# A quarter of one tile's first FFN layer as seven half-size products

## The chip, the cores and the metric

The kernel runs on one core of one Trainium2 chip. The metric is the time of one execution in device microseconds. Before the change the median of three runs is 283.71 us (283.59 to 284.48).

The engines are named as the profile names them: PE is TensorE (matrix products; PEld is its weight load), DVE is VectorE, ACT is ScalarE, POOL is GpSimd, SP is SyncE, which issues transfers.

## The reference

```python
# q, k, v: (8 batches, 8 heads, 576 tokens, 64), window 32, dilation 4
scores = q @ k.T / sqrt(64)                  # masked: heads 0..3 by (0 <= rel < 32),
attn = softmax(scores) @ v                   # heads 4..7 by (0 <= rel < 128 and rel % 4 == 0)
x = attn.transpose(0, 2, 1, 3).reshape(4608, 512)
h = maximum(x @ w_in, 0.0)                   # w_in: 512 x 2048   first FFN layer
out = (h * h) @ w_out                        # w_out: 2048 x 512  second FFN layer
```

## The kernel before, in words

**The tiles.** The 4608 tokens of the FFN are nine tiles of 512 (`NT`), counted here from 0; the seventh is tile 6 and starts at token 3072, the sixth is tile 5. Attention goes batch by batch (576 tokens) between the FFN steps, and writes its transposed result into `xT`, the FFN's input. Each later tile is 32 groups of work: 16 groups for the first layer and 16 for the second. Group 32t is the first of tile t, so tile 5 is groups 160 to 191 and tile 6 groups 192 to 223. One loop goes over all groups and builds every engine's queue in that order; tables hang other work behind a numbered group: `WEIGH_IN` (sums of pieces of `w_in`), `GATHER` (differences of pieces of `xT`) and the list `steps` (attention). Each engine runs its queue strictly in the order written.

**First layer, plain form.** `g1(u)` is four products of 128x512 (L1026) into one of the four PSUM banks of `pf`; ACT takes the bank through a relu into `h2T` (L1039); DVE squares two of these results at a time (L1042), after every odd `u`. `u` stands for feature block `u // 2` of the low half, or of the high half when `u` is odd. After `u` = 7 and `u` = 15 `add_up` (L1178) makes sums of the squared blocks for the second layer, four DVE instructions, two of which can be put off.

**First layer, seven-product form.** `unit` (L1078) computes four feature blocks (two low, two high) by seven products on half tiles instead of eight: M1, M5, M2, M6, M3, M7, M4, each of four 128x256 instructions. They use the banks of attention: X (`pa`) for M1, M6, M7 and M4, one added onto the other; Y (`po`) for M5 and M3; Z (`pd`) for M2. ACT copies what stands in the bank behind M1, M5 and M6 into buffers (L1087); DVE adds such a copy to the bank behind M2, M3 and M7 (L1186) into `h2T`. ACT then takes the relu of the low part (L1102), of one half of the high part (L1112) and, straight from the bank, of the other half behind M4 (L1114); DVE squares both parts (L1090). The seven products need four sums of pieces of `w_in` (`weigh_in`, L1456; the last pair of them is written into buffer `qb`) and four differences of pieces of `xT` (`gather`, L1464, into `x_sum`, which lies in `planes`). The kernel before uses this form in half of tile 7 (`mixed`, where units and plain groups are dealt in turn) and in all of tile 8 (`final`).

**Second layer.** `g2_fast` makes seven half-size products on 128x256 in every tile from the fourth on (L1284). In tiles 3 to 5 (`crowded`) the order is M1, M2, M6, M2, M5, M7, M3, M4, with the results taken by L1186, L1199 and L1201. In tile 6 it is M1, M5, M6, M3, M7, M2, M4.

**Attention beside it.** A visit (`quadrants`, L409) is one bundle of small products: scores of two head pairs, and the weighted values and sums of two others. It takes both `pa` banks, `po`, `pd` and up to four banks of `pf`. Visits stand behind groups 175 and 183 (tile 5, where the second is called the last bundle here) and behind 207 and 215 (tile 6). Behind a visit ACT takes exponentials (L774) and logarithms (L741, L742, L756); DVE multiplies masks (L779), adds (L782, L791) and writes the normalized result from `po`, `pf` and `pa` into `xT` (L759, L763).

Of the kernel before, what the change touches and what calls it, by code (L numbers as in the profile page):

```python
# [12 lines left out]
RES = 4  # L13
# [51 lines left out]
def kernel(  # L65
# [13 lines left out]
    NTOK = B * S  # L79
# [15 lines left out]
    NT = 512  # L95
# [1 line left out]
    XB = 2  # L97
    FAST = 3
    WEIGH = (61, 61, 62, 84, 84, 85, 85, 86)
    WEIGH_IN = (18, 19, 20, 21, 22, 23, 195, 195)  # L100
    GATHER = (219, 220, 228, 232)
    PAIRED = 4
    SPLIT = 2
    STAGE = (0, 1, 0, 2, 1, 1, 1, 1)
# [1 line left out]
    RING = 4 * S  # L106
    KT = DM // P
    NF = DFF // P
# [55 lines left out]
    x_sum = [xx[0][:, :, :].rearrange("p x y -> p (x y)")[:, NT * x : NT * x + NT] for x in range(8)]  # L164
    x_sum = [x.rearrange("p (k r m) -> p k r m", k=2, r=2) for x in x_sum]
    x_sum = x_sum[0:4], x_sum[4:8]
# [811 lines left out]
    def deal(units, others):  # L978

        out_ = []  # L980
        for x in range(0, len(others), 4):
            u = units[7 * x // 4 : 7 * x // 4 + 7]
            out_ += [*u[0:3], others[x], *u[3:5], others[x + 1], u[5], *others[x + 2 : x + 4], u[6]]
        return out_
# [7 lines left out]
    def ffn_groups(tk0: int, nt: int):  # L992
# [74 lines left out]
        def unit(step):  # L1067

            d, name = divmod(step, len(UNIT))
            name = UNIT[name]  # L1070
            bank, lhs, rhs = FIRST[name]
            if name in ("M1", "M5", "M2"):
                pool, label = {"X": (ps_a, "pa"), "Y": (ps_o, "po"), "Z": (ps_d, "pd")}[bank]
                mine[bank] = pool.tile([P, 2, HD], f32, name=label)
            to = mine[bank]
            for x in range(2):
                for k in range(2):
                    nc.tensor.matmul(  # L1078
                        to[:, x, :].rearrange("p (r m) -> p r m", r=2), lhs(2 * d + x, k), rhs(k),
                        start=x == k == 0 and name in ("M1", "M5", "M2"), stop=x == k == 1, skip_group_check=True,  # L1080
                    )
            fs = slice(2 * d, 2 * d + 2)
            low, high = (h[:, fs, :] for h in (h_last if final else (h2T[:, 0:HF], h2T[:, HF:])))

            def put_by(x):
                mine[x] = parts_of["abc".index(x) + 3 * (d % 2)]
                nc.scalar.copy(mine[x], to[:, :, :])  # L1087

            def square(h):
                nc.vector.tensor_tensor(out=h, in0=h, in1=h, op=ALU.mult)  # L1090

            if name in ("M1", "M5", "M6"):
                put_by({"M1": "c", "M5": "b", "M6": "a"}[name])
            elif name == "M2":
                plus(low[:, :, 0:HD], to[:, :, :], mine["c"])
                if final and d == HF // 4:
                    add_up(0, HF // 2, (0, 1))
                elif final and d == 1:
                    lazy.pop(0)()
            elif name == "M3":  # L1100
                plus(low[:, :, HD:], to[:, :, :], mine["a"])
                nc.scalar.activation(low, low, ACT.Relu)  # L1102
            elif name == "M7":
                plus(high[:, :, HD:], to[:, :, :], mine["b"])
                if final and d == HF // 4:
                    add_up(0, HF // 2, (2, 3))
                elif final and d < 2:
                    lazy.pop(0)()
                square(low)
                while held:  # L1110
                    held.pop(0)()
                nc.scalar.activation(high[:, :, HD:], high[:, :, HD:], ACT.Relu)  # L1112
            else:
                nc.scalar.activation(high[:, :, 0:HD], to[:, :, :], ACT.Relu)  # L1114
                while held:
                    held.pop(0)()
                if not final and d:
                    add_up(4, 8, (0,))
                elif final and d == 0:
                    lazy.pop(0)()  # L1120
                square(high)
                if final and d == HF // 2 - 1:
                    add_up(HF // 2, HF, (0, 1, 2, 3))
                elif not final and d == 0:
                    add_up(0, 2, (0, 2))
                elif not final:
                    add_up(2, 4, (0,))
                    lazy.append(lambda: (add_up(2, 4, (2,)), add_up(4, 8, (2,))))
                    lazy.append(lambda: add_up(0, 4, (3,)))
                    lazy.append(lambda: add_up(4, 8, (3,)))  # L1130
                    lazy.append(lambda: (add_up(0, 4, (1,)), add_up(4, 8, (1,))))
# [8 lines left out]
            return lambda k: xT[:, 2 * y + k, 2 * half : 2 * half + 2, g0 % gr : g0 % gr + nm]  # L1140

        def x_of(x):
            return lambda k: x_sum[int(final)][x][:, k, :, :]

        UNIT = ("M1", "M5", "M2", "M6", "M3", "M7", "M4")
        FIRST = {
# [7 lines left out]
        }  # L1154

        mixed = tk0 == NTOK - 2 * NT
        sums_at = {7: (0, 4), 15: (4, 8)} if not mixed else {}
        visited, crowded = (FAST <= tk0 // NT < x for x in (B - 1, B - 2))

        def quarter(f0, f1, high, j):  # L1160
# [6 lines left out]
        def add_up(f0, f1, which):  # L1167

            s1, s2, s4 = (x[:, f0:f1, :].rearrange("p f (i t) -> p f i t", t=P) for x in (h_sum_last if final else h_sum))
            a11, a12, a21, a22 = (quarter(f0, f1, high, j) for j in range(2) for high in range(2))  # L1170
            todo = (
                (s1, a21, a22, ALU.add),
                (a21, a11, a21, ALU.subtract),
                (s2, s1, a11, ALU.subtract),
                (s4, a12, s2, ALU.subtract),
            )
            for to, one, two_, op in (todo[x] for x in which):
                nc.vector.tensor_tensor(out=to, in0=one, in1=two_, op=op)  # L1178

        final = tk0 + nt == NTOK  # L1180
# [4 lines left out]
        def plus(to, one, two_):  # L1185
            nc.vector.tensor_tensor(out=to, in0=one, in1=two_, op=ALU.add)  # L1186
# [84 lines left out]
        def g2_fast(n):  # L1271

            lo, hi = (CUTS + [len(ITEMS)])[n : n + 2]
            if n == 0:
                for bank in "ZX" if crowded else "YX":
                    cur[bank] = ps_f.tile([P, 2, HD], f32, name="pf")
            for name, f, i, y0, y1 in ITEMS[lo:hi]:
                bank, lhs, rhs = PRODUCTS[name]
                piece = final and name == "M3"
                if piece and f == 0:  # L1280
                    cur.pop(bank, None)
                if bank not in cur:
                    cur[bank] = ps_f.tile([P, 2, HD], f32, name="pf")
                nc.tensor.matmul(  # L1284
                    cur[bank][:, i, y0:y1], lhs(f, i), rhs(f)[:, y0:y1],
                    start=f == 0 and (piece or name in fresh and i == 0), stop=f == NF // 2 - 1, skip_group_check=True,
                )
                if f < NF // 2 - 1:
                    continue
                if piece:  # L1290
                    plus(c12[:, i, y0:y1], cur[bank][:, i, y0:y1], c12[:, i, y0:y1])
                    if y1 == HD:
                        keep(2 * i, HD, DM, 1)
                elif i:
                    after(name)
# [46 lines left out]
        if final:  # L1342
            return [lambda x=x: unit(x) for x in range(len(UNIT) * HF // 2)] + [lambda n=n: g2_fast(n) for n in range(NF)]
        if mixed:
            first_ = [lambda i=i: g1(i) for i in range(NF // 2, NF)]
            second_ = [lambda x=x: unit(x) for x in range(2 * len(UNIT))]
            return deal(second_, first_) + [lambda n=n: g2_fast(n) for n in range(NF)]
        if fast:
            return [lambda i=i: g1(i) for i in range(NF)] + [lambda n=n: g2_fast(n) for n in range(NF)]
        return [lambda i=i: g1(i) for i in range(NF // per)] + [  # L1350
# [14 lines left out]
    for es, bs in ((slice(0, NE // 2), slice(0, NB)), (slice(NE // 2, NE), slice(8, NB))):  # L1365
        for hl in range(2):
            to = vbd[0][64 * hl : 64 * hl + 64, es, bs, 64 - 64 * hl : 128 - 64 * hl]
# [89 lines left out]

    def gather(x):

        to, x = x_sum[x // 2], x % 2  # L1460
        t0 = (NTOK - (2 - (to is x_sum[1])) * NT) // RES % (RING // RES)
        b11, b12, b21, b22 = (xT[:, 2 * k : 2 * k + 2, 2 * z : 2 * z + 2, t0 : t0 + P] for k in range(2) for z in range(2))
        for out_, one, two_ in (((to[0], b12, b11), (to[2], b22, b12)), ((to[1], b22, to[0]), (to[3], b21, to[1])))[x]:
            nc.vector.tensor_tensor(out=out_, in0=one, in1=two_, op=ALU.subtract)  # L1464
# [149 lines left out]
    for g, group in enumerate(groups):  # L1614
# [10 lines left out]
        for x in [x for x in range(len(WEIGH)) if WEIGH[x] == g]:  # L1625
            weigh(x)
        for x in [x for x in range(len(WEIGH_IN)) if WEIGH_IN[x] == g]:
            weigh_in(x)
        for x in [x for x in range(len(GATHER)) if GATHER[x] == g]:
            gather(x)  # L1630
# [34 lines left out]
```

## Time and profile before

| | |
|---|---|
| median of three runs | 283.71 us (283.59 to 284.48) |
| the profiled execution, its own time | 283.61 us |
| its span, first to last instruction | 281.5 us |
| granted TensorE clock | 1.000 |
| PE busy | 275.7 us (98%) |
| DVE busy | 205.8 us (73%) |
| ACT busy | 191.2 us (68%) |
| POOL busy | 122.6 us (44%) |

The span leaves out 2.1 us that lie around the instructions. Busy time of PE counts pipelined products by modelled ends, so the starts of instructions and the chain that ended last are the surer measure of its pace. A row of the timeline gives start, length, engine, line and operation, output and inputs with shapes, how many were merged and, in brackets, how long the engine had been idle and what ended that. Rows of the chain give start, length, engine, output tile, line and count; they mark the modelled start in the array, which is some 0.16 us later than the timeline's start of the same product.

### The profile page before, as it was taken

To read this page: it belongs to the slowest core of one execution; us is meant where nothing else is said; L and a number is where in the kernel's file an instruction comes from. 1 tells how busy PE (TensorE), PEld (TensorE's weight loads), DVE (VectorE), ACT (ScalarE), POOL (GpSimd) and SP (SyncE) were. 2 spreads that over 40 slices of the span, in tenths; PEclk is the share of its full clock that TensorE was granted. 3 is DMA by queue.
4 is the path that set the end of the run, shared out by engine and by line. 5 is a ranking of instruction groups with operands and counts; after the bars stand their busy time and mean duration, and the time that the engine had idled before them with its cause. 6 is when DMAs were issued, how large, how long until landed. Compare 5 with 4: busy or idle time off the path is not lost.

```text
span 281.5 us, 8766 instructions
## 1 busy us (share of the span) xinstructions
PE 275.7 (98%) x3615; PEld 204.5 (73%) x3625; DVE 205.8 (73%) x485; ACT 191.2 (68%) x386; POOL 122.6 (44%) x208
## 2 busy tenths in 40 slices
PE   8999999999999999999999999999999999999995
PEld 7689745957755585558865786578657887899984
DVE  1786644554889779689779867986787678889752
ACT  6788725786866875788756874687568648776620
POOL 8686358673672785478286849730000000000000
PEclk9999999999999999999999999999999999999999
DMA  7999999999999989999999999840400030000314
GB/s 120 193 185 191 210 192 225 215 156 170 164 216 191 168 111 188 198 181 165 147 201 197 116 170 172 135 44 2 149 2 3 2 141 10 0 2 0 112 41 149
DMA packets 85735, 36.84 MB, mean 131 GB/s; under 512 B 53312, under 2 KB 81856, under 8 KB 85696
## 3 DMA queue, kind: packets, MB, share of 16 engines
q0 software_dynamic: 49056, 18.49, 59.4%
q1 hardware_dynamic: 36496, 17.70, 32.2%
q8 instruction: 28, 0.46, 0.6%
q10 hardware_dynamic: 144, 0.10, 0.1%
q14 instruction: 11, 0.09, 0.1%
HBM read 37.50 MB, written 9.44 MB: 167 GB/s over the span
## 4 chain that ended last, share of the span: by engine, by line
PE 98%; issue 1%; ACT 0%; DVE 0%
PE pf L1026 37%; PE pf L1284 26%; PE pf L1327 14%; PE pa L1078 4%; PE po L812 2%; PE po L409 2%; PE po L1078 2%; PE pf L409 2%; PE pa L409 1%; PE pd L1327 1%; PE pa L842 1%; PE pd L1078 1%; PE pf L894 1%; PE pd L409 1%; PE pa L603 0%
## 5 line engine op out<-in xcount | busy, mean ns | idle before, releaser
L1026 PE MATMUL pf<-xT,w_in 128*128 128x512 bf16 (+1 forms) x608 | 107.5, 334 | 0.0
L1026 PEld LDWEIGHTS <-w_in 128*128 128x128 bf16 x608 | 67.3, 114 | 34.4
L1039 ACT ACTIVATE h2T<-pf 128x512 bf16<-128x512 f32 x119 | 69.5, 601 | 28.8 <-PE pf L1026 28.5
L1042 DVE TENSOR_TENSOR h2T<-h2T 128x512 bf16<-128x512 bf16 (+1 forms) x88 | 44.7, 521 | 20.7 <-ACT h2T L1039 18.6
L362 POOL DMA_DIRECT2D vbd<-in_v_dram x80 | 42.9, 547 | 27.9 <-DMA kb<-in_k_dram 11.1
L1327 PE MATMUL pf<-w_out_sb,h2T 128*128 128x512 bf16 (+1 forms) x199 | 38.8, 345 | 0.8 <-issue 0.5
L1327 PEld LDWEIGHTS <-h2T 128*128 128x128 bf16 x224 | 21.3, 98 | 17.7
L1284 PEld LDWEIGHTS <-h2T 128*128 128x128 bf16 x320 | 30.7, 98 | 3.7
L1284 PE MATMUL pf<-w_out_sb,h2T 128*128 128x256 bf16 x160 | 19.6, 273 | 0.0
L1284 PE MATMUL pf<-kb,h2T 128*128 128x256 bf16 x160 | 19.6, 273 | 0.0
L1284 PE MATMUL pf<-qb,qb 128*128 128x256 bf16 x160 | 19.1, 273 | 0.0
L1284 PEld LDWEIGHTS <-qb 128*128 128x128 bf16 x160 | 15.7, 98 | 1.8
L756 ACT ACTIVATE rec<-rec 128x576 f32<-128x576 f32 x24 | 16.2, 697 | 0.5
L216 POOL DMA_DIRECT2D kb<-in_k_dram x19 | 13.1, 690 | 7.1 <-DMA w_in<-in_moe_w_in_dram 2.3
L238 POOL DMA_DIRECT2D vbd<-in_v_dram x16 | 11.0, 687 | 11.2 <-DMA kb<-in_k_dram 7.2
L216 POOL DMA_DIRECT2D qb<-in_q_dram x19 | 13.4, 705 | 4.5 <-DMA qb<-in_q_dram 1.4
L1186 DVE TENSOR_TENSOR whole<-pf,whole 128x512 f32<-128x512 f32 x18 | 12.3, 686 | 3.3 <-PE pf L1284 2.6
L354 POOL DMA_DIRECT2D vbd<-in_v_dram x20 | 12.0, 616 | 5.3 <-DMA qb<-in_q_dram 2.7
L774 ACT ACTIVATE pt<-pa 128x384 bf16<-128x384 f32 (+1 forms) x24 | 11.0, 493 | 4.8 <-DVE xT L763 4.1
L348 POOL DMA_DIRECT2D vd<-in_v_dram x20 | 12.1, 619 | 1.1 <-DMA vbd<-in_v_dram 1.0
L759 DVE TENSOR_TENSOR xT<-pf,rec 128x512 bf16<-128x512 f32 x12 | 8.3, 688 | 4.7 <-ACT rec L756 4.7
L409 PEld LDWEIGHTS <-vbd 64*64 64x64 bf16 x328 | 8.8, 107 | 3.4 <-issue 3.3
(226 smaller groups left out, 516.2 us busy)
## 6 DMA issues: line engine op xcount, KB each, us to landing
out_dram<-whole SPq DMA_DIRECT2D x14, 256.0 KB, 4.6
out_dram<-whole SPq DMA_DIRECT2D x5, 512.0 KB, 3.6
qb<-in_q_dram POOLq DMA_DIRECT2D x7, 320.0 KB, 9.5
kb<-in_k_dram POOLq DMA_DIRECT2D x7, 320.0 KB, 8.3
vd<-in_v_dram POOLq DMA_DIRECT2D x34, 64.0 KB, 5.7
w_out_sb<-in_moe_w_out_dram POOLq DMA_DIRECT2D x4, 512.0 KB, 10.9
out_dram<-whole SPq DMA_DIRECT2D x16, 128.0 KB, 5.8
qb<-in_q_dram POOLq DMA_DIRECT2D x6, 256.0 KB, 5.9
```

Source lines behind the costliest of these rows:

```text
L216: nc.gpsimd.dma_start(t[p0 : p0 + n, part, h0:h1, :], src[b, h0:h1, t0 : t0 + RES * n, :].rearrange("h (p r) d -> p h (r d)", r=RES),)
L348: nc.gpsimd.dma_start(vds[b][rows, e, :, :], v[b, H // 2 + 2 * e + (hl ^ crossed(b, e + NE // 2)), 0:512, :].rearrange("(m p r) d -> p m ( ...
L362: nc.gpsimd.dma_start(v_rows[b % 2][p0 + 16 * r : p0 + 16 * r + 16, e, :, :], v[b, 2 * e + hl, :, :].rearrange("(i m r) d -> r m i d", r=R ...
L409: nc.tensor.matmul(out, lhs, rhs, start=begin, stop=True, skip_group_check=True)
L756: nc.scalar.activation(rec[:, :], rec[:, :], ACT.Exp, scale=-1.0)
L1026: nc.tensor.matmul(to, w_in_sb[piece][:, kt, c0 : c0 + 509 : 4], rhs, start=(kt == kts[0] and x == 0), stop=(kt == kts[-1] and x == per - ...
L1039: nc.scalar.activation(hv, acc[u][:, :].rearrange("p (x n) -> p x n", x=per), ACT.Relu)
L1042: nc.vector.tensor_tensor(out=hv, in0=hv, in1=hv, op=ALU.mult)
L1078: nc.tensor.matmul(to[:, x, :].rearrange("p (r m) -> p r m", r=2), lhs(2 * d + x, k), rhs(k), start=x == k == 0 and name in ("M1", "M5", " ...
L1186: nc.vector.tensor_tensor(out=to, in0=one, in1=two_, op=ALU.add)
L1284: nc.tensor.matmul(cur[bank][:, i, y0:y1], lhs(f, i), rhs(f)[:, y0:y1], start=f == 0 and (piece or name in fresh and i == 0), stop=f == NF ...
L1327: nc.tensor.matmul(cur[m][:, a0:a1], h2[:, f, P * m : P * m + P], w_out_sb[:, f, a0:a1], start=(f == 0 and a0 == c0), stop=(f == NF - 1), ...
```

## The change

Tile 6 now computes its first four feature blocks (the former `g1(0)` to `g1(3)`, 16 products of 128x512) by one `unit` of seven products (28 of 128x256). The units stand between the plain groups in the order g1(4), g1(5), M1 M5, g1(6), M2 M6, g1(7), M3 M7, g1(8), g1(9), M4, g1(10) to g1(15); M1 and M5 share a group, so tile 6 still has 32 groups. Its first `add_up` moves from behind `u` = 7 to behind M4. Two gathers for tile 6 are added behind group 190. The last two sums of `w_in` move from behind group 195 (tile 6) to behind group 182, ahead of the visit behind group 183.

```diff
-    WEIGH_IN = (18, 19, 20, 21, 22, 23, 195, 195)
-    GATHER = (219, 220, 228, 232)
+    WEIGH_IN = (18, 19, 20, 21, 22, 23, 182, 182)
+    GATHER = (219, 220, 228, 232, 190, 190)
...
                 nc.scalar.activation(high[:, :, 0:HD], to[:, :, :], ACT.Relu)
                 while held:
                     held.pop(0)()
+                if thin:
+                    square(high)
+                    add_up(0, 4, (0, 1, 2, 3))
+                    return
...
-            return lambda k: x_sum[int(final)][x][:, k, :, :]
+            return lambda k: x_sum[int(not mixed)][x][:, k, :, :]
...
-        sums_at = {7: (0, 4), 15: (4, 8)} if not mixed else {}
+        thin = tk0 == NTOK - 3 * NT
+        sums_at = {} if mixed else {15: (4, 8)} if thin else {7: (0, 4), 15: (4, 8)}
...
+        if thin:
+            plain_ = iter(range(4, NF))
+            order = [x or (next(plain_),) for x in ((), (), "01", (), "23", (), "45", (), (), "6", *((),) * 6)]
+            return [
+                lambda x=x: [unit(int(y)) for y in x] if isinstance(x, str) else g1(*x) for x in order
+            ] + [lambda n=n: g2_fast(n) for n in range(NF)]
...
-        to, x = x_sum[x // 2], x % 2
-        t0 = (NTOK - (2 - (to is x_sum[1])) * NT) // RES % (RING // RES)
+        to, t0, x = x_sum[(0, 1, 1)[x // 2]], (NTOK - (2, 1, 3)[x // 2] * NT) // RES % (RING // RES), x % 2
```

Three places show how the queues change. Line numbers from L1114 on are higher after the change by 4 to 11: L1186 becomes L1191, L1178 L1183, L1456 L1467, L1464 L1474.

The first is DVE's queue in tile 5, around the masks (L779) of the visit behind group 183. Before:

```order
L1186 TENSOR_TENSOR whole_109<-pf_3964,whole_109 128x2x256
L779 TENSOR_TENSOR pt_4167<-pt_4167,mask_n_87 128x448
L779 TENSOR_TENSOR pt_4167<-pt_4167,mask_n_87 128x384
L791 TENSOR_TENSOR kbd_102<-pt_4167 128x128
L791 TENSOR_TENSOR kbd_102<-pt_4167 128x96
L1186 TENSOR_TENSOR whole_109<-pf_4177,whole_109 128x2x256
```

The same place in DVE's queue after the change:

```order
L1191 TENSOR_TENSOR whole_109<-pf_3964,whole_109 128x2x256
L1467 TENSOR_TENSOR qb1_97<-w_in0_89,w_in_sum1_107 128x2x512
L1467 TENSOR_TENSOR qb1_97<-w_in512_90,w_in_sum1_107 128x2x512
L779 TENSOR_TENSOR pt_4169<-pt_4169,mask_n_87 128x448
L779 TENSOR_TENSOR pt_4169<-pt_4169,mask_n_87 128x384
L791 TENSOR_TENSOR kbd_102<-pt_4169 128x128
L791 TENSOR_TENSOR kbd_102<-pt_4169 128x96
L1191 TENSOR_TENSOR whole_109<-pf_4179,whole_109 128x2x256
```

The two sums of `w_in` now stand between the second-layer result that M2 completes and the masks.

The second place is DVE's queue from the end of tile 5 into the first layer of tile 6; `whole` takes the last result of tile 5's second layer, `kbd` takes keys of attention, `h2T` is the first layer's result. Before:

```order
L782 TENSOR_TENSOR kbd_102<-pt_4218 128x128
L1186 TENSOR_TENSOR whole_109<-pf_4177,whole_109 128x2x256
L1042 TENSOR_TENSOR h2T_105<-h2T_105 128x2x512
L380 COPY kbd_102<-planes_101 64x4x5x16 x2
L1042 TENSOR_TENSOR h2T_105<-h2T_105 128x2x512
L1456 TENSOR_TENSOR qb1_97<-w_in0_89,w_in_sum1_107 128x2x512
L1456 TENSOR_TENSOR qb1_97<-w_in512_90,w_in_sum1_107 128x2x512
L380 COPY kbd_102<-planes_101 64x4x4x16 x2
L1042 TENSOR_TENSOR h2T_105<-h2T_105 128x2x512 x2
L1178 TENSOR_TENSOR qb2_99<-h2T_105 128x1024
```

After, with the results of M2, M3 and M7 taken from `pd`, `po` and `pa`:

```order
L782 TENSOR_TENSOR kbd_102<-pt_4220 128x128
L1474 TENSOR_TENSOR planes_101<-xT_94 128x512 x2
L1474 TENSOR_TENSOR planes_101<-xT_94,planes_101 128x512 x2
L1191 TENSOR_TENSOR whole_109<-pf_4179,whole_109 128x2x256
L1042 TENSOR_TENSOR h2T_105<-h2T_105 128x2x512
L380 COPY kbd_102<-planes_101 64x4x5x16 x2
L380 COPY kbd_102<-planes_101 64x4x4x16
L1191 TENSOR_TENSOR h2T_105<-pd_4288,kb1_98 128x2x256
L380 COPY kbd_102<-planes_101 64x4x4x16
L1042 TENSOR_TENSOR h2T_105<-h2T_105 128x2x512
L1191 TENSOR_TENSOR h2T_105<-po_4274,kb1_98 128x2x256
L1191 TENSOR_TENSOR h2T_105<-pa_4268,kb1_98 128x2x256
```

The four gathers stand ahead of tile 5's last result, and the two results of M3 and M7 stand behind the square of g1(7).

The third place is ACT's queue in the first layer of tile 6, which before is sixteen relus (L1039) in a row. After, from behind the relu of g1(5):

```order
L1087 COPY kb1_98<-pa_4268 128x512
L1087 COPY kb1_98<-po_4274 128x512
L1039 ACTIVATE h2T_105<-pf_4281 128x512
L1087 COPY kb1_98<-pa_4268 128x512
L1039 ACTIVATE h2T_105<-pf_4300 128x512
L1102 ACTIVATE h2T_105<-h2T_105 128x1024
L1112 ACTIVATE h2T_105<-h2T_105 128x2x256
L1039 ACTIVATE h2T_105<-pf_4320 128x512
L1039 ACTIVATE h2T_105<-pf_4326 128x512
L1114 ACTIVATE h2T_105<-pa_4268 128x2x256
```

Six instructions of the unit replace four relus, and the relus of g1(8) and g1(9) (`pf_4320`, `pf_4326`) stand behind two of them that wait for DVE.

## The prediction

> **What bounds the kernel now.** I read the page first, then the waits of PE, then the stretch that the change touches, group by group.
>
> ```profile
> PE 275.7 (98%) x3615; PEld 204.5 (73%) x3625; DVE 205.8 (73%) x485; ACT 191.2 (68%) x386; POOL 122.6 (44%) x208
> PE 98%; issue 1%; ACT 0%; DVE 0%
> PE po L812 <- DVE kbd L1361: 1.1, 1, 1.1
> PE pf L894 <- issue: 0.6, 1, 0.6
> PE pf L1327 <- issue: 0.5, 3, 0.2
> 200.05:213.90 13.85, 13.85 (x66) 7.18 (x64) 10.32 (x20) 8.96 (x15) 0.00 (x0) 1.00 0.16 58
> 215.10:228.30 13.20, 13.20 (x187) 11.66 (x178) 10.21 (x27) 8.16 (x18) 0.00 (x0) 1.00 0.07 23
> ```
>
> The first two lines are the page's engines and its chain that ended last; 98% of the chain is PE. The next three are all the waits of PE in the whole execution: five, none in lines that tiles 5 to 8 run. The last two are windows over tile 6's first layer and its second (PE, PEld, DVE, ACT, POOL, granted clock, transfers): PE is busy throughout at clock 1.00, DVE for 10.3 of 13.9 us, ACT for 9.0. So from here to the end the time is PE's issue time, and a wait can only be added. Whatever PE saves ends the kernel sooner, one for one; whatever PE waits is lost the same way.
>
> **The products.** These are rows of the chain, the first over tile 6's first layer, the others at the ends of the stretch of tile 7 in which units and plain groups are dealt.
>
> ```profile
> 200.21 13.81 PE pf L1026 x64
> ...
> 228.46 0.44 PE pa L1078 x4
> 228.90 0.44 PE po L1078 x4
> ...
> 241.05 0.87 PE pa L1078 x8
> ```
>
> A plain product costs 13.81 / 64 = 0.2158 us. Between 228.46 and 241.05 there stand 13 units and 8 plain groups: (12.59 - 32 x 0.2158) / 13 = 0.437 us for a unit of four, or 0.1093 us a half product. Removed: 16 x 0.2158 = 3.45 us. Added: 7 x 0.437 = 3.06 us. PE's issue time falls by 0.39 us. That is all that can be gained, since nothing else on PE changes.
>
> The nearest row that could make half products dearer is their weight load.
>
> ```profile
> L1078 PEld LDWEIGHTS <-w_in_sum x72: 111/113/116, 228.6 to 263.8; 128*128 128x128 bf16 x72
> ```
>
> A load takes 113 ns. Were that the pace, 28 of them would take 3.16 us and the gain be 0.29; the chain's 0.1093 says that they run beside the products. Below nothing the price can't go. I take 0.39.
>
> The Trainium skill speaks against this change on the page "TensorE: Matmul & The Clock Gate", section "Back-to-back issue gap": in a stream of weight loads and products the spacing is set by both, some 81 ns at 128 columns and 131 ns at 512. A straight line between these gives an estimate of 98 ns at 256 columns, by which 28 half products would cost 2.74 us against 2.10 for the 16 and the change would lose 0.64. The trace disagrees here: 216 and 109 ns, in proportion to the columns.
>
> **The two sums of w_in.** These are DVE's rows around their new place and the row of their old one.
>
> ```profile
> 193.04 0.68 DVE L1186 TENSOR_TENSOR whole<-pf,whole 128x512 f32<-128x512 f32 x1
> 194.78 0.74 DVE L779 TENSOR_TENSOR pt<-pt,mask_n 128x448 bf16<-128x448 bf16 x2 [1.06 <-ACT pt L774]
> 195.56 0.34 DVE L791 TENSOR_TENSOR kbd<-pt 128x128 bf16<-128x128 bf16 x2
> 196.76 0.69 DVE L1186 TENSOR_TENSOR whole<-pf,whole 128x512 f32<-128x512 f32 x1 [0.85 <-PE pf L1284]
> 204.94 1.29 DVE L1456 TENSOR_TENSOR qb<-w_in,w_in_sum 128x1024 bf16<-128x1024 bf16 x2
> ```
>
> They take 1.29 us from about 193.65, where DVE sat idle for 1.06; the masks start some 0.15 late and the 0.85 us of idle time behind them takes that up. By 196.76 nothing is late: price nothing. Were that cover gone, only masks that PE needs behind group 207, 20 us later, would be late. Their inputs have been in place since tile 0, and the buffer's earlier contents were transposed for batch 7 long before.
>
> **The gathers.** The end of tile 5 on DVE, ACT's relu of the second plain group, and the four gathers that tile 7 has already:
>
> ```profile
> 200.07 0.23 DVE L782 TENSOR_TENSOR kbd<-pt 128x128 bf16<-128x128 bf16 x1
> 200.25 0.69 DVE L1186 TENSOR_TENSOR whole<-pf,whole 128x512 f32<-128x512 f32 x1
> 202.60 0.69 DVE L1042 TENSOR_TENSOR h2T<-h2T 128x1024 bf16<-128x1024 bf16 x1 [1.66 <-ACT h2T L1039]
> 201.98 0.60 ACT L1039 ACTIVATE h2T<-pf 128x512 bf16<-128x512 f32 x1 [0.27 <-PE pf L1026]
> 226.82 0.76 DVE L1464 TENSOR_TENSOR planes<-xT 128x512 bf16<-128x512 bf16 x2
> 227.50 0.88 DVE L1464 TENSOR_TENSOR planes<-xT,planes 128x512 bf16<-128x512 bf16 x2
> 228.29 0.68 DVE L1186 TENSOR_TENSOR whole<-pf,whole 128x512 f32<-128x512 f32 x1
> ```
>
> Four gathers delay what follows by 228.29 - 226.82 = 1.47 us. From 200.25 they end at about 201.7; tile 5's last result follows and ends at 202.4, ahead of the square that starts at 202.60: the idle 1.66 us hides them. M5, the first to read a gather, has its turn at 200.05 + 8 x 0.2158 + 0.437 = 202.21, M6, M7 and M4 later. The bank of that last result is next used by g1(8), at 206.1. Price nothing; without the cover the squares would be late and count in what follows.
>
> **A new wait of PE, at M4.** M4 adds onto bank X, so it has to wait until DVE has read M7's result from there. DVE takes M3's and M7's results behind the square of g1(7). The second plain group is issued by 200.05 + 8 x 0.2158 = 201.78 and its square starts at 202.60, 0.82 later. In the new order g1(7) is issued by 200.05 + 16 x 0.2158 + 4 x 0.437 = 205.25, so its square starts at 206.07. Then the queue's pace counts:
>
> ```profile
> 204.33 0.69 DVE L1042 TENSOR_TENSOR h2T<-h2T 128x1024 bf16<-128x1024 bf16 x1 [0.64 <-ACT h2T L1039]
> 231.78 0.69 DVE L1186 TENSOR_TENSOR h2T<-po,kb 128x512 bf16<-128x512 f32 x1 [0.56 <-ACT kb L1087]
> 232.50 1.06 ACT L1102 ACTIVATE h2T<-h2T 128x1024 bf16<-128x1024 bf16 x1 [0.76 <-DVE h2T L1186]
> 233.47 0.58 ACT L1039 ACTIVATE h2T<-pf 128x512 bf16<-128x512 f32 x1
> 233.94 0.62 ACT L1112 ACTIVATE h2T<-h2T 128x512 bf16<-128x512 bf16 x1
> 234.47 1.07 ACT L1039 ACTIVATE h2T<-pf 128x512 bf16<-128x512 f32 x2
> 235.42 0.61 ACT L1114 ACTIVATE h2T<-pa 128x512 bf16<-128x512 f32 x1
> ```
>
> A square 0.69 long is followed after 0.61 (204.33 to 204.94). So M3's result is taken at 206.68 and M7's at 207.29, which ends at 207.98. PE reaches M4 at 205.25 + 2 x 0.437 + 8 x 0.2158 = 207.85. It waits 0.13 us and the hand-over. No row shows PE waiting for DVE in these tiles; from DVE to ACT it is 232.50 - (231.78 + 0.69) = 0.03. Bounds: nothing, if M7's result comes 0.13 earlier than worked out, and 0.3, if the hand-over costs as much as that from PE to ACT (201.98 - 201.78 = 0.20). I take 0.15, nearest to the row from DVE. Behind M4 on PE stand g1(10) to g1(15) and all the rest.
>
> **What then is late.** ACT's relu of the low part waits for M3's result (207.37) and starts at 207.40. By tile 7's paces (0.97 behind it, 0.53 behind L1112, 0.95 for two plain relus) the relu of g1(8) starts at 208.90, that of g1(9) at 209.38, M4's at 209.85. g1(12) needs the bank of g1(8), free at 209.5; its turn is at 207.85 + 0.15 + 0.44 + 1.73 = 210.17. No wait there, 0.67 to spare. On DVE the square of g1(9) then starts at 210.0, that of the high part at 210.6, and the four sums of `add_up` behind it:
>
> ```profile
> 208.51 0.69 DVE L1178 TENSOR_TENSOR qb<-h2T 128x1024 bf16<-128x1024 bf16 x1
> 211.18 1.29 DVE L1042 TENSOR_TENSOR h2T<-h2T 128x1024 bf16<-128x1024 bf16 x2
> 215.15 0.69 DVE L1178 TENSOR_TENSOR qb<-h2T 128x1024 bf16<-128x1024 bf16 x1
> 216.84 0.69 DVE L759 TENSOR_TENSOR xT<-pf,rec 128x512 bf16<-128x512 f32 x1 [0.27 <-ACT rec L756]
> 220.38 0.23 DVE L782 TENSOR_TENSOR kbd<-pt 128x128 bf16<-128x128 bf16 x1
> 220.81 0.69 DVE L759 TENSOR_TENSOR xT<-po,rec 128x512 bf16<-128x512 f32 x1 [0.20 <-ACT rec L756]
> 221.42 0.21 DVE L763 TENSOR_TENSOR xT<-pa,rec 128x64 bf16<-128x64 f32 x1
> 222.31 0.15 PE po L409
> ```
>
> They begin at about 211.3 instead of 208.51 and take the same 2.67 us (to 211.18), so they end at 214.0. Two double squares (1.2), two single ones (0.4 each) and two sums (1.3) follow without a pause, and the result at 216.84 starts at about 217.4: 0.55 late. The row of 220.38 moves to 220.9 and the last two to 221.1 and 221.7, ending at 221.9. They free `po` and `pa` for the visit behind group 215, which PE begins at 222.31 before and at 222.07 when 0.24 us sooner. Of 0.7 us to spare (222.31 - 221.63) 0.1 to 0.2 is left. Second-layer products that read the late squares and sums have theirs in time: the last block of M1 is read seven eighths through its 1.75 us, at 216.5, and squared by 216.0. Price nothing, but with little to spare.
>
> **The sum**, against the profiled execution's own 283.61 us: 283.61 - 0.39 + 0.15 = 283.37. The median of the runs shown is 0.10 above that execution; the same offset gives 283.47. I forecast 283.4 us, a change of about -0.1%.
>
> **Rivals.**
>
> *The new wait doesn't come.* If M7's result is read 0.13 us sooner, all of the gain stays: 283.22 us. For it: the margin is smaller than the differences of single rows. Against: the square of g1(7) stands ahead of both results and its start follows PE with a fixed 0.82. Chance 0.25.
>
> *DVE's lateness reaches the visit behind group 215* (the other side). PE waits there for `po` and `pa` one for one, once DVE is more than 0.15 later than worked out. From 0.4 more the kernel is slower than before; from 1.25 more it is slower by over 0.3%. The price is bounded by letting none of the some 20 instructions from the high part's square on overlap its neighbour: 20 x 0.08 = 1.6 us, and 283.37 + 1.45 = 284.8 us. For it: 0.55 us of the 0.7 are gone by my own working, and ACT's share of the chain rests on tile 7's paces. Against: DVE's rows overlap everywhere, and nothing else is added behind M4. Chance 0.15, of which 0.11 beyond 0.3%.
>
> *Half products are paced by their weight load.* Then 283.61 - 0.29 + 0.15 = 283.47 us. For it: 113 ns of load against 109 of pace. Against: tile 7's chain with the same operands. Chance 0.06. The page's own figures would take it to the slower side; that the chain shows a pace in proportion to the columns leaves it no more.
>
> **How the numbers follow.** My forecast has 0.50, and 0.04 stays for a gain that I don't see; 0.39 us is 0.14%, so faster by over 0.3% (0.85 us, about what a measurement of this kernel can tell from no change) has only that 0.04. Within 0.3% lie the forecast, the first and third rivals and the small part of the second: 0.85. Slower: 0.11. The range starts at the full gain off the lowest run, 283.59 - 0.39, less the 0.1 between execution and median: 283.1. It ends at the forecast's gain off the highest run, 284.48 - 0.24 = 284.2, which takes in the second rival up to 0.8 us of waiting. Left out are 0.15.
>
> **What would show it.** In the profile after: 28 products of L1078 in tile 6 at 0.437 us a unit; one wait of PE at M4 for DVE's result from `pa`, 0.1 to 0.3 us long, or none; the two sums of w_in and the four gathers inside what was idle on DVE; the visit behind group 215 some 0.24 us sooner and DVE's last result of `po` ending just ahead of it. I am wrong if PE waits anywhere else in tiles 5 to 7, if a unit costs more than 0.45 us, or if the time leaves 283.1 to 284.2.

## The result and the profile after

| | median, us | lowest to highest | ratio to the kernel before, 95% interval |
|---|---|---|---|
| changed kernel, first comparison | 283.18 (before: 283.80) | 282.83 to 289.16 | 0.9974 [0.9963, 0.9985] |
| the same, second comparison | 283.60 (before: 283.73) | 282.89 to 288.70 | 0.9994 [0.9972, 1.0016] |
| the same, third comparison | 283.66 (before: 283.68) | 282.90 to 288.10 | 0.9998 [0.9970, 1.0027] |
| kernel before against itself | 283.91 (283.73) | 283.54 to 285.25 | 1.0001 [0.9978, 1.0025] |

The first comparison says 0.6 us faster, the two that followed say no difference. The time alone doesn't settle a change of this size, so I read the traces from one fixed row to another. One part of the time no row shows, what lies outside the span: it is 1.72 to 1.82 us in 22 runs of the changed kernel and 2.09 to 2.22 us in 34 of the kernel before, so some 0.37 us less. The profiled execution of the first comparison was a disturbed one (289.16 us, with early waits for transfers), so what follows is the profile of the same kernel in the second: 283.28 us, span 281.5.

Its page and its windows over tile 6's first and second layer (PE, PEld, DVE, ACT, POOL, granted clock, transfers):

```profile
PE 277.0 (98%) x3637; PEld 206.0 (73%) x3637; DVE 209.4 (74%) x492; ACT 191.9 (68%) x388; POOL 122.5 (44%) x208
200.05:213.66 13.61, 13.60 (x78) 8.41 (x76) 10.63 (x22) 9.63 (x17) 0.00 (x0) 1.00 0.17 60
214.86:228.08 13.22, 13.22 (x188) 11.69 (x179) 11.07 (x28) 8.07 (x18) 0.00 (x0) 1.00 0.07 22
```

The first layer takes 13.61 us instead of 13.85. ACT has 388 instructions instead of 386; that will matter. The chain over tile 6, to the first unit of tile 7:

```profile
200.21 1.73 PE pf L1026 x8
201.94 0.44 PE pa L1078 x4
202.37 0.44 PE po L1078 x4
...
206.28 1.73 PE pf L1026 x8
208.02 0.60 PE pa L1078 x4
...
222.09 0.15 PE po L409
...
228.24 0.44 PE pa L1078 x4
```

One of the unit's seven products (four instructions) takes 0.44 us and M4 0.60: 0.16 of it is the wait. The visit behind group 215 begins at 222.09 (222.31 before) and tile 7's first unit at 228.24 (228.46). In both kernels tile 6 begins at 200.21, so 0.22 us are gained. DVE's timeline says what M4 waits for, and what stands just ahead of the visit:

```profile
206.07 0.69 DVE L1042 TENSOR_TENSOR h2T<-h2T 128x1024 bf16<-128x1024 bf16 x1 [0.94 <-ACT h2T L1039]
206.69 0.68 DVE L1191 TENSOR_TENSOR h2T<-po,kb 128x512 bf16<-128x512 f32 x1
207.29 0.68 DVE L1191 TENSOR_TENSOR h2T<-pa,kb 128x512 bf16<-128x512 f32 x1
...
221.58 0.21 DVE L763 TENSOR_TENSOR xT<-pa,rec 128x64 bf16<-128x64 f32 x1
```

M7's result ends at 207.97. The chain's row of M4 holds four products, 0.44 us, and the rest up to 0.60 is spent on that result. The row from `pa` ends at 221.79, 0.22 ahead of the visit's start on the timeline (222.01): no wait.

The 0.22 us stay up to the last unit (of seven products) of tile 8. The chain from there to the last result, first before:

```profile
262.23 0.44 PE pa L1078 x4
...
263.75 0.44 PE pa L1078 x4
...
265.50 0.44 PE pa L1078 x4
265.94 12.35 PE pf L1284 x120
...
278.31 0.29 DVE h2T L1186
```

And after:

```profile
262.00 0.44 PE pa L1078 x4
...
263.53 0.51 PE pa L1078 x4
...
265.36 0.60 PE pa L1078 x4
265.96 12.38 PE pf L1289 x120
...
278.37 0.29 DVE h2T L1191
```

The three rows of `pa` are M6, M7 and M4. M6 is 0.23 sooner, M7 takes 0.07 longer, M4 0.16, and the last result is 0.06 later than before. From tile 6's first product to it: 278.31 - 200.21 = 78.10 us before, 278.37 - 200.21 = 78.16 after. The whole gain inside the span is given back in one unit. The list of PE's waits, on which the prediction relied, shows none of this:

```profile
PE po L812 <- DVE kbd L1372: 1.1, 1, 1.1
```

This is its only row after; waits as short as 0.07 and 0.16 us stand only in the chain's durations. M7 adds onto the bank that ACT's copy of M6 reads, and M4 waits for DVE's result of M7. ACT's copy, that result and, by the timeline, M7 and M4 on PE, first before:

```profile
262.75 0.59 ACT L1087 COPY kb<-pa 128x512 f32<-128x512 f32 x1 [0.89 <-PE pa L1078]
264.58 0.68 DVE L1186 TENSOR_TENSOR vbd<-pa,qb 128x512 bf16<-128x512 f32 x1
263.59 0.60 PE L1078 MATMUL pa<-planes,w_in_sum 128*128 128x256 bf16 x4
265.34 0.60 PE L1078 MATMUL pa<-planes,w_in 128*128 128x256 bf16 x4
```

After:

```profile
262.81 0.59 ACT L1087 COPY kb<-pa 128x512 f32<-128x512 f32 x1 [1.17 <-PE pa L1078]
264.63 0.68 DVE L1191 TENSOR_TENSOR vbd<-pa,qb 128x512 bf16<-128x512 f32 x1
263.44 0.60 PE L1078 MATMUL pa<-planes,w_in_sum 128*128 128x256 bf16 x4
265.36 0.60 PE L1078 MATMUL pa<-planes,w_in 128*128 128x256 bf16 x4
```

M6 starts 0.23 sooner, but its copy 0.06 later: 0.81 us behind M6's start instead of 0.52. ACT was idle for 1.17 us ahead of it. The trace also has a row for the semaphore on which ACT waits there. It ends 0.04 us before the copy starts in the kernel before, and 0.32 us before it after. So the copy's input was there, and ACT did nothing for 0.32 us. After, M7 starts 0.05 us behind the end of the copy and M4 0.05 behind the end of M7's result; before, 0.25 and 0.08. So 0.20 and 0.03 us were to spare there.

### The profile page after: what moved, and what is told of

Its sections match the earlier page's. It is cut to its first block, busy times and chain, and to the rows that moved or that the text cites. A ratio compares the mean times of both kernels' runs of the same rounds, so it can differ in the third digit from the quotient of the medians.

```text
span 287.4 us, 8798 instructions
## 1 busy us (share of the span) xinstructions
PE 278.3 (97%) x3627; PEld 206.3 (72%) x3637; DVE 208.4 (73%) x492; ACT 192.1 (67%) x388; POOL 122.4 (43%) x208
## 4 chain that ended last, share of the span: by engine, by line
PE 79%; DMA 15%; POOL 4%; issue 1%; ACT 0%; DVE 0%; POOLq 0%
PE pf L1026 28%; PE pf L1289 26%; PE pf L1332 11%; DMA w_out_sb<-in_moe_w_out_dram 6%; PE pa L1078 4%; DMA kb<-in_k_dram 4%; DMA w_in<-in_moe_w_in_dram 3%; PE po L1078 2%; DMA vbd<-in_v_dram 2%; PE pf L409 2%; PE po L409 2%; PE pa L409 1%; PE pd L1332 1%; PE pd L1078 1%; POOL qb L216 1%
## 5 line engine op out<-in xcount | busy, mean ns | idle before, releaser
L1026 PE MATMUL pf<-xT,w_in 128*128 128x512 bf16 (+1 forms) x592 | 104.9, 333 | 0.4 <-DMA w_in<-in_moe_w_in_dram 0.3
L1026 PEld LDWEIGHTS <-w_in 128*128 128x128 bf16 x592 | 65.3, 114 | 32.8 <-DMA w_in<-in_moe_w_in_dram 1.0
L1039 ACT ACTIVATE h2T<-pf 128x512 bf16<-128x512 f32 x115 | 66.8, 601 | 26.6 <-PE pf L1026 26.3
L1042 DVE TENSOR_TENSOR h2T<-h2T 128x512 bf16<-128x512 bf16 (+1 forms) x86 | 43.2, 517 | 19.7 <-ACT h2T L1039 18.2
L1332 PE MATMUL pf<-w_out_sb,h2T 128*128 128x512 bf16 (+1 forms) x199 | 40.6, 355 | 1.0 <-issue 0.5
L1191 DVE TENSOR_TENSOR whole<-pf,whole 128x512 f32<-128x512 f32 x18 | 12.4, 686 | 2.9 <-PE pf L1289 2.6
```

What stands on the lines that cost most here:

```text
L1026: nc.tensor.matmul(to, w_in_sb[piece][:, kt, c0 : c0 + 509 : 4], rhs, start=(kt == kts[0] and x == 0), stop=(kt == kts[-1] and x == per - ...
L1039: nc.scalar.activation(hv, acc[u][:, :].rearrange("p (x n) -> p x n", x=per), ACT.Relu)
L1042: nc.vector.tensor_tensor(out=hv, in0=hv, in1=hv, op=ALU.mult)
L1332: nc.tensor.matmul(cur[m][:, a0:a1], h2[:, f, P * m : P * m + P], w_out_sb[:, f, a0:a1], start=(f == 0 and a0 == c0), stop=(f == NF - 1), ...
```

## The experiments

"The stretch" is the time from tile 6's first product to the last result, in the chain of one profiled execution each; "M6 to copy" is read in the last unit of tile 8. (Several expectations below count a stretch from tile 3's first product: 164.00 us in the kernel before.) The runs with 21, 66 and 130 more are one execution each, of 284.76, 290.72 and 296.83 us; all but 0.3 us of what they take longer than 283.61 lies ahead of tile 6.

| kernel | ACT instructions | tile 6 to tile 7's first unit | the stretch | M6 to copy |
|---|---|---|---|---|
| before | 386 | 28.25 | 78.10 | 0.52 |
| changed | 388 | 28.03 | 78.16 | 0.81 |
| sums and gathers only | 386 | 28.25 | 78.09 | 0.53 |
| M4 one group later | 388 | 28.39 | 78.52 | 0.81 |
| changed, one ACT instruction more | 389 | 28.03 | 77.87 | 0.53 |
| before, two more | 388 | 28.25 | 78.37 | 0.81 |
| before, 21 more | 407 | 28.25 | 78.10 | (second unit: 0.80) |
| before, 66 more | 452 | 28.25 | 78.10 | 0.53 |
| before, 130 more | 516 | 28.25 | 78.39 | 0.82 |
| both losses mended | 389 | 27.86 | 77.70 | 0.53 |

**Both kernels again, unchanged.**

> The changed kernel once more. Two theories. Theory A: the change is worth what its products and its one new wait give, 0.39 - 0.17 = 0.22 us (ratio 0.9992), and the 0.7 us first measured is scatter of the early transfers (the runs of before reach from 283.2 to 285.3). Theory B: it is worth 0.5 to 1.0 us (ratio 0.9965 to 0.9982), and the rest comes from somewhere outside tile 6's first layer. Both expect 28 products of L1078 in tile 6 at 0.437 us a unit and one wait of PE of 0.17 us ahead of M4. A expects the span from tile 2's first product to the end shorter by 0.22 us; B expects 0.5 us or more there, in a stage that a comparison of the two traces names.

> The kernel before, unchanged, against itself: what this way of measuring gives for no change at all. Both theories expect a ratio of 1.000. Theory A expects an interval at least 0.001 wide to either side, or a median that differs by 0.2 us or more between equal kernels; theory B expects the two within 0.1 us.

Measured: 0.9994 [0.9972, 1.0016] for the changed kernel and 1.0001 [0.9978, 1.0025] for the kernel before. The stretch of the second execution of before is 78.10 us, as in the first. What differs between executions lies ahead of tile 6: it begins at 200.21 and 200.48 us in these two, and at 206.08 in the profile of the first comparison, whose stretch is still 78.15. The kernel before against itself came out as theory A expected. For the change both theories missed: A's 0.22 us is there up to tile 8 and gone at the last result, and B's 0.5 us is in no stage of the trace; the 0.37 us that come off lie outside the span.

**Sums and gathers only.** The kernel before with the two sums of `w_in` behind group 182 and the four gathers behind 190, whose results nothing reads; tile 6 has no unit.

```diff
-    WEIGH_IN = (18, 19, 20, 21, 22, 23, 195, 195)
-    GATHER = (219, 220, 228, 232)
+    WEIGH_IN = (18, 19, 20, 21, 22, 23, 182, 182)
+    GATHER = (219, 220, 228, 232, 190, 190)
```

> The kernel before with only VectorE's part of the change: the last two sums of w_in behind group 182, and the two added gathers behind group 190, whose results nothing reads here; all 16 plain products of tile 6 stay. Theory A: PE never waits for this work, ratio 1.000 (no change within 0.1 us). Theory B, in the form that the moved sums free something on PE: 0.3 to 0.5 us faster (ratio 0.998 to 0.999).

Measured: 283.34 us, 0.9980 [0.9959, 1.0001]; stretch 78.09. The moved and added work costs PE nothing, as forecast. The median is 0.39 us lower all the same, with a stretch that is the same to 0.01 us: some 0.2 us of it lie outside the span (1.96 us in the median of its runs), the rest ahead of tile 6 or in the scatter of the runs.

**M4 one group later.** The changed kernel with M4 behind g1(10).

```diff
-((), (), "01", (), "23", (), "45", (), (), "6", *((),) * 6)
+((), (), "01", (), "23", (), "45", (), (), (), "6", *((),) * 5)
```

> The changed kernel with M4 one plain group later (behind g1(10) instead of g1(9)). Theory A: PE reaches M4 0.86 us later, the wait of 0.17 us is gone and no other comes, 0.39 us faster than before (ratio 0.9986) and 0.17 us faster than the changed kernel; VectorE's sums start some 0.1 us later at most, and the visit behind group 215 still begins without a wait. Theory B expects the same 0.17 us step on top of a larger gain.

Measured: 283.80 us, 1.0001 [0.9982, 1.0020]. From tile 6's first product to tile 7's first unit it takes 28.39 us. Its chain at M4, and its row in the waits of PE:

```profile
207.86 2.59 PE pf L1026 x12
210.45 0.44 PE pa L1078 x4
PE po L409 <- DVE xT L763: 0.3, 1, 0.3
```

M4 takes 0.44 us: the wait is gone. But DVE's work behind M4 is then one group later, and the visit behind group 215 waits 0.3 us for it. So theory A missed: tile 6 takes 0.14 us longer than before, not 0.39 less. The prediction's second rival is real and lies one group away.

**One ACT instruction more.** The changed kernel; a copy that builds a mask at the start is cut in two.

```diff
-            put(mask_d[:, 704:768], mk[:, 96:160])
+            put(mask_d[:, 704:736], mk[:, 96:128])
+            put(mask_d[:, 736:768], mk[:, 128:160])
```

> The changed kernel with one more ACT instruction: a copy of 64 columns that builds a mask at the start is made as two copies of 32, in time in which nothing waits for ACT. From tile 3's first product to the last result the kernel before took 164.00 and 164.06 us in two executions, the changed kernel 164.05 and 164.06: it is 0.22 to 0.23 ahead up to the last unit of tile 8 and loses that there, where ACT's copy behind M6 starts 0.32 us after its wait has ended. Theory C: the 0.32 us is a pause of ACT at a fixed place in its list of instructions (the copy is number 448, that is 7 x 64, counted from 0 with the waits), and the change put that copy onto the place by adding two instructions. Then with one more the wait stands at the place, where nothing is lost: the copy starts 0.04 us after its wait, M7 and M4 of the last unit wait no longer than before, and the stretch is 163.83 us (163.80 to 163.88). Theory D: the pause belongs to this unit and to what runs beside it when everything is 0.23 sooner (a store, DVE's earlier results). Then it stays at 0.32 us and the stretch is 164.05. The whole time differs by 0.2 us between the two, less than the rounds can tell.

Measured: 283.30 us, 0.9983 [0.9957, 1.0008]. M6, M7, M4 and the last result in its chain, and ACT's copy:

```profile
262.73 0.44 PE pa L1078 x4
...
264.26 0.44 PE pa L1078 x4
...
266.00 0.44 PE pa L1078 x4
...
278.81 0.29 DVE h2T L1191
263.26 0.58 ACT L1087 COPY kb<-pa 128x512 f32<-128x512 f32 x1 [0.89 <-PE pa L1078]
```

The copy follows M6 by 0.53 us, M7 and M4 take 0.44, the stretch is 77.87: the forecast's 0.24 gained, measured 0.23. From tile 3 it takes 163.78 us, 0.02 below the range that theory C gave. Theory D falls, since nothing near the unit was touched.

**The kernel before with two more.** The same copy cut in three, and nothing of the change.

> The kernel before with two more ACT instructions: the same mask copy as three. Nothing of the change is in it. Theory C: ACT's copy behind M6 in the last unit of tile 8 becomes number 448 and starts 0.32 us after its wait, instead of 0.04; M7 and M4 on PE come some 0.07 and 0.16 later, and the stretch from tile 3's first product to the last result grows from 164.00 to 164.06 to 164.23 to 164.30. Theory D: no pause, since PE is where it was before; the stretch stays at 164.00 to 164.06.

Measured: 284.10 us, 1.0025 [0.9995, 1.0056]. The same rows:

```profile
262.39 0.44 PE pa L1078 x4
...
263.92 0.51 PE pa L1078 x4
...
265.75 0.60 PE pa L1078 x4
263.20 0.58 ACT L1087 COPY kb<-pa 128x512 f32<-128x512 f32 x1 [1.17 <-PE pa L1078]
```

M7 with 0.51 and M4 with 0.60 are those of the changed kernel. Two short copies at the start cost 0.27 us at the end: the stretch is 78.37 (164.27 from tile 3, as theory C expected).

**Which places in the list pause.** Cutting the copy in 22 puts number 448 on the copy of M6 in tile 8's second unit; 66 more put number 512, 130 more number 576 on the last unit's. (Numbers count from 0 through ACT's program, waits included, and a branch at its start that the profile doesn't list.) Only mask copies were cut; this is the cut in 22:

```diff
-            put(mask_d[:, 704:768], mk[:, 96:160])
+            for c in range(704, 768, 3):
+                put(mask_d[:, c : min(c + 3, 768)], mk[:, c - 608 : min(c + 3, 768) - 608])
```

> The kernel before with 66 more ACT instructions, all in the building of masks at the start: one copy of 64 columns becomes 64 copies of one, another four. ACT's copy behind M6 in the last unit of tile 8 is then number 512 (8 x 64) of its list. Theory C64: ACT pauses wherever a multiple of 64 falls on the instruction just behind a wait. Then the copy starts 0.32 us after its wait, as in the changed kernel, and from tile 6's first product to the last result it takes 78.37 us (as with two more), not 78.10. Theory C448: only number 448 of the list, or something else that two more instructions brought about, gives the pause. Then the copy starts 0.04 us after its wait and the stretch is 78.10 us.

> The kernel before with 21 more ACT instructions (the same mask copy as 22). Number 448 is now ACT's copy behind M6 in another unit, the second of tile 8's four. Theory C64 and C448 alike: the pause of 0.32 us goes there and the last unit has none. What it costs there depends on what PE has to spare: between nothing and the 0.27 us that it cost in the last unit, so the stretch is 78.10 to 78.37 us. Theory D (the pause belongs to the last unit and to its moment): no pause in the second unit.

> The kernel before with 130 more ACT instructions, again in the building of masks at the start. ACT's copy behind M6 in the last unit of tile 8 is then number 576 = 448 + 128 of its list. In the runs so far number 448 gave the pause wherever it stood behind a wait (the last unit or the second one of tile 8) and number 512 gave none; and the last 8 KB transfer on the instruction queue 14 started when ACT stood at about number 448 (264.04 us, 252.82 and 237.10 in kernels in which that number lies at different places). Theory R: ACT gets its instructions in pieces of 128, asks for the next at numbers 64 + 128 n, and pauses there for 0.32 us. Then the copy starts 0.32 us after its wait and from tile 6's first product to the last result it takes 78.37 us. Theory C448: only that one number pauses; then 0.04 us and 78.10 us.

Measured, with 66 more (the last unit's M6 in the chain, then its copy):

```profile
269.30 0.44 PE pa L1078 x4
269.83 0.59 ACT L1087 COPY kb<-pa 128x512 f32<-128x512 f32 x1 [0.89 <-PE pa L1078]
```

No pause at number 512, and a stretch of 78.10: C64 falls. With 21 more, in the second unit:

```profile
251.36 0.44 PE pa L1078 x4
252.16 0.59 ACT L1087 COPY kb<-pa 128x512 f32<-128x512 f32 x1 [1.07 <-PE pa L1078]
253.10 0.44 PE pa L1078 x4
```

The pause is there (0.80 from M6 to the copy, 0.32 behind the wait). It costs nothing, because eight products of the second layer stand between M3 and M7 in that unit (six in the last one) and M7 keeps its 0.44; the stretch is 78.10. With 130 more, in the last unit:

```profile
275.13 0.44 PE pa L1078 x4
276.66 0.53 PE pa L1078 x4
278.51 0.60 PE pa L1078 x4
275.95 0.59 ACT L1087 COPY kb<-pa 128x512 f32<-128x512 f32 x1 [1.18 <-PE pa L1078]
```

At number 576 the pause is back, 0.33 us behind the wait, and the stretch is 78.39. So numbers 448 and 576 pause and 512 doesn't, as theory R says; its other numbers (64, 192, 320) were not tried. That the pause is the request for the next instructions is argued from the transfers on queue 14 alone, not shown.

**Both losses mended.** One ACT instruction more, and the square of g1(7) put behind M7's result in DVE's queue.

```diff
-                if mixed:
+                if mixed or thin and u == 7:
                     held.append(square)
...
+                if thin:
+                    held.pop(0)()
                 square(low)
```

> The changed kernel with the one ACT instruction more, and with DVE's queue in tile 6 altered: the results of M3 and M7 stand ahead of the square of g1(7), not behind it. Taking C and the prediction's term for M4 together, both losses go and the whole saving on PE is left: no wait of PE at M4 (0.17 us in the changed kernel), no pause in tile 8's last unit, and 164.03 - 0.39 = 163.64 us for the stretch (163.6 to 163.7); against the runs of the kernel before 0.9986. Rival: DVE or ACT is then late elsewhere (the visit behind group 215, the relu of g1(8)), and PE waits there 0.1 to 0.2 us: 163.75 to 163.9. By theory D the pause in tile 8 stays: 163.87.

> The version with both losses mended, once more. From tile 6's first product to the last result its profiled execution took 77.70 us against 78.10 in the kernel before and 78.16 in the changed kernel, and the whole time in the rounds was 0.9982 [0.9961, 1.0002] of the kernel before. If the 0.40 us shows in the whole time, the ratio is 0.9986 again, within the 0.2% that two sets of runs of one kernel differ by; a ratio above 1.0005 would say that the rest of the kernel gives the 0.40 us back where the profile doesn't look.

Measured: 283.25 us, 0.9982 [0.9961, 1.0002]; again 283.27 us, 0.9975 [0.9953, 0.9996]. DVE's timeline around M4 and M4 itself in the chain:

```profile
206.09 0.69 DVE L1193 TENSOR_TENSOR h2T<-po,kb 128x512 bf16<-128x512 f32 x1 [0.81 <-ACT kb L1087]
206.70 0.68 DVE L1193 TENSOR_TENSOR h2T<-pa,kb 128x512 bf16<-128x512 f32 x1
207.30 0.68 DVE L1042 TENSOR_TENSOR h2T<-h2T 128x1024 bf16<-128x1024 bf16 x1
208.16 0.44 PE pa L1078 x4
```

M7's result now ends at 207.38, 0.6 ahead of M4 (208.00 on the timeline). Tile 6 takes 27.86 us, 0.39 less than before, and the stretch 77.70 in both executions: 0.40 less than before and 0.46 less than the changed kernel. This is the version to keep. With the 0.37 us outside the span (1.77 and 1.78 in its profiles) it is 0.77 us faster, a ratio of 0.9973, which both intervals hold. One part of its expectation missed: from tile 3 it takes 163.72 us in the first execution and 164.79 in the second, where 163.64 was expected. What is too much was lost between tile 3 and tile 4 (0.13 and 1.19 us), which the edit doesn't touch.

**The changed kernel a third time.**

> The changed kernel unchanged, with five rounds more. The first comparison gave 0.9974 [0.9963, 0.9985] against the kernel before, the second 0.9994 [0.9972, 1.0016], while the stretch from tile 3's first product to the end is the same in all profiled executions of the two. If the 0.7 us of the first comparison came from executions that differ ahead of tile 3, this one gives 0.998 to 1.001 and a stretch of 164.05 us. If the change does gain 0.5 to 1.0 us ahead of tile 3, it gives 0.9965 to 0.9985 again.

Measured: 0.9998 [0.9970, 1.0027], stretch 78.15. The 0.6 us of the first comparison doesn't come back. From tile 3 this execution takes 164.95 us, so the expected 164.05 missed: 0.9 us were lost between tile 3 and tile 4, in instructions that the change doesn't touch.

## Why the prediction was right inside tile 6 and wrong about the rest

**The products.** Right. Seven times four half-size products for 16 whole ones save 0.39 us: the mended version shows 28.25 - 27.86 = 0.39. By the estimate from the sustained figures of the Trainium skill's page "TensorE: Matmul & The Clock Gate", section "Back-to-back issue gap", the change would have lost 0.64 us there; the runs disagree with it as the trace of before did.

**The wait at M4.** Right in place and size: 0.15 forecast, 0.16 measured, behind DVE's M7 result, which was worked out to end at 207.98 and ended at 207.97. The first rival (no wait) didn't come.

**Sums, gathers, lateness.** Right. PE waits nowhere for them, and the visit behind group 215 finds its banks free with 0.22 us to spare where 0.1 to 0.2 was forecast. One group later they would not have been, as the run with M4 one group later showed.

**Half products paced by their load.** No: 0.44 us for four in every row where PE doesn't wait.

**"From here to the end the time is PE's issue time ... whatever PE saves ends the kernel sooner, one for one."** This step failed. The 0.22 us that tile 6 gained reached tile 8 and were lost behind M6 of its last unit: from tile 7's first unit to the last result the changed kernel takes 0.28 us longer. M7 waits 0.07 us for ACT's late copy and M4 0.16 for the result that follows from it. I had followed the wait list (no wait of PE in tiles 5 to 8 before) and checked what the edit makes late inside tile 6. What I left out is that the edit adds two instructions to ACT's list (six for four relus) and so moves every later ACT instruction by two places. In the kernel before, the place of the pause, number 448, is the relu L1112, which starts at 265.29, 0.03 us behind the DVE result that it waits for, so no pause shows (that the 1.06 us of L1102 ahead of it hide one is likely, not shown). With two instructions more it is the copy of M6, behind which M7 and M4 had only 0.20 and 0.03 us to spare. No row of before shows that pause; the order of the queues shows the two places, and nothing in the prediction priced them; its signs of being wrong looked for waits in tiles 5 to 7 alone. The page's chain of 98% PE was true and said nothing about how little was to spare there.

**The time.** Forecast 283.4 us, a change of -0.24 us or -0.1%. The sum also carried the 2.1 us outside the span over unchanged, without a reason. Inside the span the change costs 0.06 us, outside it saves some 0.37: together -0.31 us, a ratio of 0.9989. That this lies near the forecast is luck: a loss of 0.28 us and a gain of 0.37 that the sum didn't hold nearly cancel. The second and third comparison (0.9994, 0.9998) agree with 0.9989; the interval of the first, 0.9963 to 0.9985, doesn't hold it. The rest lies inside the span, whose median is 281.4 us in its runs of the changed kernel and 281.7 in those of the two others. I can't name its cause: profiled executions of one kernel differ ahead of tile 6 by 0.3 to 1.5 us, but no trace is kept of the runs that made up that median. The bound of 0.3% for what can be told from no change was about right: the intervals were 0.1 to 0.3% either way.

## What to carry to other kernels

Where a change is worth 0.1%, compare the time between two fixed rows of the chain, behind the last place where transfers are awaited: from tile 6 it repeated to 0.01 us here (from tile 3 the changed kernel gave 164.05, 164.06 and 164.95), while whole executions differed by 0.2% with the same stretch. Then compare what lies outside the span, which can change too. An edit that adds or removes instructions on an engine moves everything behind them in that engine's list; if a gain vanishes far from the edit, look there for an engine that starts late although its wait has ended, and add or take away one harmless instruction as a test. A bank that is freed just in time is freed too late one group further on, so an order that looks better for one wait has to be followed to the next visit.

## What the hardware showed that I had not expected

ACT pauses for 0.32 us behind a wait when the instruction there is number 448 or 576 of its list, in seven executions of five kernels, to 0.02 us; at number 512 it doesn't, and at number 448 of the kernel before (L1112) no pause shows. The last transfer of 8 KB on the instruction queue 14 within the span starts at 264.04, 252.82 and 276.68 us in three of these, 1.2, 0.7 and 0.7 us after the instruction that paused. In the kernel before it starts at 263.84, ahead of number 448 (265.29). The Trainium skill (page "Perfetto Trace Analysis", section "Per-instruction lifecycle: what the profiler-reported window actually captures") gives an instruction 64 bytes, by which 8 KB would be 128 instructions, an estimate. The runs agree in so far as the two numbers that pause lie 128 apart.

What lies outside the span is 1.72 to 1.83 us in all 95 runs of the four kernels in which tile 6 has the unit, 1.83 to 2.10 with the sums and gathers only, and 2.08 to 2.23 in the others. The profiles of the first kind show one more 8 KB transfer on queue 14, 0.3 to 0.7 us behind the last instruction (282.15 in the changed kernel), that of sums and gathers shows it 1.9 us behind, and those of the others show none. What links the two stays open.
